# Sigmoid attention and a sigmoid-GELU MLP on one core: the first 512 tokens' x kept on chip, the left-over score step moved in among the previous unit's products with v, and decoding steps ranked by their load

## The chip, the cores and the metric

The kernel runs on one core of one Trainium2 chip. Its time is device microseconds of one execution, and the number that counts is the median of several runs. Beside the timed runs there is one execution under the hardware profiler; its instructions are what the profile shows.

The engines carry the profile's names: PE is TensorE's matmul, PEld its weight load, DVE is VectorE, ACT is ScalarE, SP is the engine from whose queue all DMAs are issued here.

## The reference

```
# q, k, v: (8, 12, 448, 64); w_in: (768, 2048); w_out: (2048, 768)
scores = q @ k.T / 8 - log(448)
attn   = sigmoid(scores) @ v                      # per batch and head
x      = attn, heads side by side                 # (3584, 768)
h      = x @ w_in
out    = (h * sigmoid(1.702 * h)) @ w_out
```

All of it is float32. The weights arrive as 64-bit words and are turned into float32 on chip.

## The kernel before, in words

**A planner writes the order.** The kernel first makes a list of tasks (`Plan.task`, line 101), each with an engine, a cost in microseconds, the tasks it depends on and the buffers it uses. `Plan.run` (line 113) then plays the list through by those costs and emits the instructions of each engine in the order that comes out. On the chip each engine works through its queue in that order and does not look past an instruction that waits. TensorE follows units of tasks in a given order: attention's are `side`, the rest `main`. ACT, DVE and SP pick, among the tasks that can begin, the one of the lowest key (line 226). A task's key is the place of its earliest user in the TensorE order (`keys`, line 278); `plan.early` sets the key of a listed task to half a place ahead of another one (line 141). A task of a higher key is put off when one of a lower key that is already on offer begins within 0.8 of its cost (lines 227 to 233). A task whose buffer has no slot yet may begin only when its key is within 14 places (`HORIZON`) of what TensorE is doing, unless it is marked `anytime` (line 166).

**Attention** (`attention`, line 701) has 48 pairs of heads (8 batches of 6) in 24 units of two pairs, so four heads. A pair's q and k come as one raw tile (`qkraw`, 5 buffers, loads at L432). DVE and ACT split it into a rounded part and a remainder (L458/L459 and L464, tiles `qk`, 2 buffers). The 448 keys make three chunks of 128 and 64 left over. A unit runs on TensorE, before the change, as

1. six score chunks, three per pair (`scores`, L593: three terms of two matmuls on 64x128 tiles of the array), each followed by a sigmoid on ACT (L579, tile `a`);
2. the left-over scores of all four heads (`scores_left`, L609: 64x64 tiles, straight from the two raw tiles), with their sigmoid into `al`, which has one buffer;
3. four products of score chunks with v (`values`, L626), the left-over's product (`values_left`, L639), and two more of L626. The first three chunks go to one v result, the last three to the other, and the left-over's product adds to both.

PSUM has four pairs of banks in attention, q0 to q3, and `two_banks(place)` (line 571) gives them out by place modulo 4. Before the change a unit's places are: score chunks 1 to 6, left-over 7, v results 8 and 9. So the left-over takes the banks of the third chunk, the first v result those of the fourth, and the fourth chunk of the next unit those of this unit's second v result.

`to_x` (line 656) empties a v result: ACT copies one half (L668) and DVE adds the other (L671) into a buffer `x32` of 448 tokens. A batch has 448 tokens and a block of the MLP 512, so every row of x is stored to DRAM (`xd`) in one or two parts, block by block. `make_x` (line 683) loads block 0's two halves of x back in three pieces each and splits them into rounded part and remainder (L458, L464). All other blocks are read back later.

**Decoding** (`decode`, line 476) takes 16 weight tiles from 64-bit words to float32. It goes on during attention: one load for every 2.9 pairs (`PACE`), two buffers of raw words, then seven to eight steps on DVE and ACT (L499 to L522), of which two take DVE 1.75 us each. Before the change a decoding step's key comes from the first use of its weights, which is in the MLP.

**The MLP** follows. `first_block` (line 811) does tokens 0 to 511 as plain products. The other six blocks go in two groups of three through a fast matrix scheme with fewer products (`triple`, line 951). All its matmuls stand at L799. The first weight pieces are split in `pieces` (line 817); the first two are marked `anytime`.

Of the kernel before, what the change touches and what calls it, by code (L numbers as in the profile page):

```python
# [19 lines left out]
P = 128  # L20
T = 512
# [3 lines left out]
WARM = 26  # L25

# [310 lines left out]
def sigmoid_attention_mlp(ctx: ExitStack, tc: tile.TileContext, qk, v, w, out):  # L337
# [138 lines left out]
    def decode(n):  # L476
# [47 lines left out]
        t_m.anytime = True  # L524
        decoded[n] = [Node(f, held(f, f"w32_{n}", NW_EL, k * NW_EL), [t_p]) for k in range(2)]
# [5 lines left out]
    spill = {n: [dram.tile([P, NJ, T], F32, name=f"xd{n}_{k}", tag=f"xd{n}_{k}") for k in range(2)] for n in range(NB)}  # L531
# [36 lines left out]

    place_of = {}
# [31 lines left out]
    def scores_left(n, sources, place):  # L601
# [12 lines left out]
        t = task("PE", 0.9, emit, [t for ts, _ in sources for t in ts], [ps, *(b for _, b in sources)])  # L614
        return t, sigmoid(f"a{n}_{NC}", a, ps, t, "al"), a

    def values(n, c, t_a, a, t_v, vr, ps):
# [13 lines left out]
        return task("PE", 0.76, emit, [t_a, t_v], [ps, a, vr])  # L631
# [23 lines left out]

    def to_x(b, p, ends, pair):

        xb = buffer("x32")
# [6 lines left out]
        for k, (t, ps) in enumerate(zip(ends, pair)):  # L665
            def lower(k=k, ps=ps):
                rows()
                nc.scalar.copy(xb.tile[:, k], ps.tile[:, 1, :S])  # L668

            c = task("ACT", act(S), lower, [t], [xb, ps])  # L670
            done.append(task("DVE", dve(S), lambda k=k, ps=ps: nc.vector.tensor_tensor(  # L671
                xb.tile[:, k], ps.tile[:, 0, :S], xb.tile[:, k], op=ALU.add), [c], [xb, ps]))
        copies.extend(done)
        for block, into, cols in places(b):
            for js in ([slice(0, 2)] if p % NJ < NJ - 1 else [slice(0, 1), slice(1, 2)]):
# [7 lines left out]
    def make_x(block, k):  # L683
        x = buffer("pair")
        n = NJ * T

        def first():
            if x.tile is None:
                make(x, "pair", [P, 2, 4, T], F32R, f"x{block}_{k}")

        t = [dma(lambda j=j: x.tile[:, 1, j].bitcast(F32), lambda j=j: spill[block][k][:, j], P * T * 4 / 1024,
                 spilled[block, k * NJ + j], [x], first) for j in range(NJ)]
        xs[block, k] = (round_and_rest(
            (act(n), cast(n), dve(n)), x, lambda: x.tile[:, 1, :NJ].bitcast(F32), t, [],
            lambda: x.tile[:, 0, :NJ], lambda: x.tile[:, 1, :NJ],
        ), x)
# [4 lines left out]
    def attention():  # L701
# [7 lines left out]
        units, held_ = [], 1  # L709
        for n, (b, p) in enumerate(pairs):  # L710
            t_q, qkr, t_v, vr = load_pair(b, p)
            t_s, s = split_pair(b, p, t_q, qkr)
            firsts.append(t_s)
            if n % 2:
                left = scores_left(n, [first, (t_q, qkr)], held_ + (7 if n > 1 else NC + 1))
            at = held_ + 1 + n % 2 * NC + (n == 1)
            chunks = [scores(n, c, [t_s] if n else t_q[: c + 1], s, at + c) for c in range(NC)]
            if n % 2 == 0:
                first, chunks0, pair0 = (t_q, qkr), chunks, (b, p)
                continue  # L720
            held_ += 9
            pair = [two_banks(held_ - 1), two_banks(held_)]
            both = [values(m, c, got[1], got[2], t_v, vr, pair[m % 2])
                    for m, cs in ((n - 1, chunks0), (n, chunks)) for c, got in enumerate(cs)]
            both.insert(NC + 1, values_left(*left[1:], t_v, vr, pair))
            copied = len(copies)
            to_x(*pair0, [both[NC + 1], both[-1]], pair)
            run = [t for t, _, _ in chunks0 + chunks]
            plan.early += [(t, run[1]) for t in urgent]
            urgent[:] = copies[copied:]  # L730
# [601 lines left out]
```

## Time and profile before

| what | us |
|---|---|
| timed runs | 1045.62, 1046.72, 1048.9 (median 1046.72) |
| the profiled execution's own time | 1042.55 |
| its span, first to last instruction | 1040.8 |
| PE busy | 1032.8 |
| DVE busy | 863.7 |
| ACT busy | 552.9 |
| matmuls of the MLP (L799), four groups of rows | 327.5 + 327.2 + 66.5 + 66.4 |
| products with v (L626) | 117.8 |
| score chunks (L593, split q and k) | 93.9 |

The granted clock of TensorE was 0.999. Busy times of different engines overlap, so they do not add up to the span. PE's ends are modelled, and matmuls overlap in the array, so a busy PE says little; where TensorE loses time, the starts of its instructions say more. A row of the timeline gives the start, the length until the last end, the engine, the line, the operation with its tiles, how many instructions were merged, and in brackets the idle time before it with what ended that. The rows of windows give, for a stretch, its length and each engine's busy time with the count of instructions in it.

### The profile page before, as it was taken

The numbers are of one execution on the slowest core, as the hardware profiler recorded it, in microseconds if no ns is written. First come the engines' busy times: TensorE is split into PE (matmuls) and PEld (weight loads), VectorE is DVE, ScalarE is ACT, GpSimd is POOL, SyncE is SP. The second block draws the span as 40 slices with busy tenths as digits, with TensorE's granted clock in tenths as the row PEclk, the third lists the DMA queues.
The fourth block names the chain that finished last, engine by engine and source line by source line (L and its number), as shares of the span: only waits on it lengthen the run. The fifth ranks groups of instructions, "written<-read, shape, count | busy, mean of one in ns | idle before, by whom it ended". The sixth has DMA issues, their size and how long they took to land.

```text
span 1040.8 us, 14831 instructions
## 1 busy us (share of the span) xinstructions
PE 1032.8 (99%) x5876; PEld 784.3 (75%) x5876; DVE 863.7 (83%) x792; ACT 552.9 (53%) x537; POOL 0.2 (0%) x4
## 2 busy tenths in 40 slices
PE   9999999999999999999999999999999999999998
PEld 5555555555888888888888888888888888888886
DVE  5999899984998857978998999889985658899856
ACT  6999889886655623435563443431325564233432
POOL 0000000000000000000000000000000000000000
PEclk9999999999999999999999999999999999999999
DMA  9999999973899998756676657878865555645466
GB/s 357 362 380 369 326 345 334 337 269 139 333 374 355 385 381 297 246 192 215 225 240 195 210 181 235 258 246 299 311 226 204 183 181 162 202 153 157 137 195 238
DMA packets 114708, 271.50 MB, mean 261 GB/s; under 512 B 10320, under 2 KB 80080, under 8 KB 112592
## 3 DMA queue, kind: packets, MB, share of 16 engines
q1 hardware_dynamic: 114640, 270.57, 74.8%
q8 instruction: 46, 0.75, 0.3%
q14 instruction: 22, 0.18, 0.0%
HBM read 185.60 MB, written 84.93 MB: 260 GB/s over the span
## 4 chain that ended last, share of the span: by engine, by line
PE 94%; DVE 2%; ACT 1%; DMA 1%; issue 1%; SPq 0%; ACTq 0%; DVEq 0%
PE p L799 63%; PE av L626 9%; PE sc L593 7%; PE h L799 6%; PE o_q L799 6%; PE sc L609 2%; PE av L639 1%; DMA qkraw<-qk 0%; DVE x L671 0%; ACT a L579 0%; DMA xd<-x 0%; ACT sign L503 0%; DVE w L522 0%; DVE qk L464 0%; DVE w L520 0%
## 5 line engine op out<-in xcount | busy, mean ns | idle before, releaser
L799 PE MATMUL p<-xp,w 128*128 128x512 f32 x1440 | 327.5, 389 | 0.1
L799 PE MATMUL p<-gp,w 128*128 128x512 f32 x1440 | 327.2, 389 | 0.0
L799 PEld LDWEIGHTS p<-xp,w 128*128 128x128 f32 x1440 | 270.2, 188 | 56.6 <-issue 0.5
L799 PEld LDWEIGHTS p<-gp,w 128*128 128x128 f32 x1440 | 270.3, 188 | 56.1
L579 ACT ACTIVATE a<-sc,bias 128x896 f32<-128x896 f32 x168 | 154.1, 1025 | 7.5 <-PE sc L593 7.3
L626 PE MATMUL av<-a,vraw 64*64 64x448 f32 x1152 | 117.8, 539 | 0.0
L593 PEld LDWEIGHTS sc<-qk 64*128 64x128 f32 x846 | 77.1, 184 | 26.5 <-issue 16.2
L593 PE MATMUL sc<-qk 64*128 64x448 f32 x846 | 93.9, 370 | 1.7 <-DVE qk L464 1.0
L626 PEld LDWEIGHTS av<-a,vraw 64*64 64x64 f32 x1152 | 42.2, 133 | 68.0 <-issue 48.3
L1197 ACT COPY h<-p 128x2048 f32<-128x2048 f32 x23 | 42.9, 1877 | 82.5 <-PE p L799 79.9
L1026 DVE TENSOR_TENSOR gp<-h,gp 128x2048 fp32r<-128x2048 f32 x27 | 61.8, 2287 | 6.8 <-ACT gp L1014 6.4
L799 PE MATMUL h<-x,w 128*128 128x512 f32 x288 | 66.5, 389 | 0.0
L799 PE MATMUL o_q<-g,w 128*128 128x512 f32 x288 | 66.4, 389 | 0.0
L1014 ACT CAST gp<-h 128x2048 fp32r<-128x2048 f32 x17 | 32.6, 1915 | 58.3 <-PE p L799 56.7
L799 PEld LDWEIGHTS h<-x,w 128*128 128x128 f32 x288 | 54.0, 188 | 11.9 <-DVE x L671 0.7
L799 PEld LDWEIGHTS o_q<-g,w 128*128 128x128 f32 x288 | 54.1, 188 | 11.2
L1231 DVE TENSOR_TENSOR h<-h,p 128x2048 f32<-128x2048 f32 x23 | 52.0, 2282 | 6.5 <-PE p L799 5.6
L1197 ACT COPY o<-p 128x1536 f32<-128x1536 f32 x18 | 25.7, 1445 | 55.3 <-PE p L799 55.1
L671 DVE TENSOR_TENSOR x<-av,x 128x448 f32<-128x448 f32 x48 | 29.9, 624 | 28.4 <-ACT x L668 28.1
L762 ACT CAST wc<-ws 128x384 fp32r<-128x384 f32 (+1 forms) x59 | 33.2, 577 | 37.4 <-DVE ws L742 19.4
L464 DVE TENSOR_TENSOR qk<-qkraw,qk 128x896 fp32r<-128x896 f32 x47 | 50.4, 1086 | 0.5
L1231 DVE TENSOR_TENSOR o<-o,p 128x1536 f32<-128x1536 f32 x18 | 31.3, 1751 | 13.9 <-PE p L799 12.9
(110 smaller groups left out, 1031.4 us busy)
## 6 DMA issues: line engine op xcount, KB each, us to landing
w<-c SPq DMA_DIRECT2D x140, 384.0 KB, 4.3
w<-c SPq DMA_DIRECT2D x52, 768.0 KB, 4.3
w<-w SPq DMA_DIRECT2D x16, 1536.0 KB, 9.4
c<-wc SPq DMA_DIRECT2D x56, 384.0 KB, 4.7
qkraw<-qk SPq DMA_DIRECT2D x47, 448.0 KB, 6.0
vraw<-v SPq DMA_DIRECT2D x24, 448.0 KB, 6.9
c<-wc SPq DMA_DIRECT2D x14, 768.0 KB, 5.0
c<-w SPq DMA_DIRECT2D x28, 384.0 KB, 3.9
```

What stands on the lines that cost most here:

```text
L464: lambda: nc.vector.tensor_tensor(lo(), src(), hi().bitcast(F32), op=ALU.subtract),
L579: nc.scalar.activation(a.tile, ps.tile[:, :, :S], AF.Sigmoid, bias=bias, scale=scale)
L593: nc.tensor.matmul(ps.tile[:, j, :S], lhsT=src[kk][rows, S + c * P : S + (c + 1) * P], rhs=src[qq][rows, :S], start=i == 0, stop=i == len( ...
L609: nc.tensor.matmul(ps.tile[cols, j, :S], lhsT=src.tile[rows, S + NC * P :], rhs=src.tile[rows, :S], start=True, stop=True, skip_group_chec ...
L626: nc.tensor.matmul(ps.tile[cols, h, :S], lhsT=vr.tile[rows, at : at + D], rhs=a.tile[rows, j], start=c == 0, stop=c == NC - 1 and (n % 2 = ...
L671: done.append(task("DVE", dve(S), lambda k=k, ps=ps: nc.vector.tensor_tensor(xb.tile[:, k], ps.tile[:, 0, :S], xb.tile[:, k], op=ALU.add), ...
L762: t_hi = on_either((act(n), lambda: nc.scalar.copy(into()[:, 0], node.view())), (cast(n), lambda: nc.vector.tensor_copy(into()[:, 0], node ...
L799: nc.tensor.matmul(ps, lhsT=ws[:, a, c * P : (c + 1) * P], rhs=x[:, d, k], start=start and i == 0 and j == 0, stop=stop and i == len(todo) ...
L1014: t_hi = on_either((act(n), lambda: nc.scalar.copy(part(0)(), node.view())), (cast(n), lambda: nc.vector.tensor_copy(part(0)(), node.view())),
L1026: nc.vector.tensor_tensor(part(1)(), node.view(), part(0)().bitcast(F32), op=ALU.subtract)
L1197: t = on_either((act(self.n), lambda: nc.scalar.copy(view(), node.view())), (dve(self.n), lambda: nc.vector.tensor_copy(view(), node.view())),
L1231: nc.vector.tensor_tensor(view(), x.view(), y.view(), op=ALU.add if s0 == s else ALU.subtract)
```

## The change

Three things change at once.

1. **x of the first 512 tokens stays on chip.** Batch 0's rows, and the first 64 tokens of batch 1, are added straight into two slots (`x_kept`), and `make_x` splits them from there. No `xd` tile exists for block 0. Batch 1's rows are added in two parts: 64 tokens into the slot, 384 into `x32`.
2. **The next unit's left-over scores** are run between this unit's `values_left` and its last two `values`. The first unit runs its own as before, the last one has none to run. PSUM places become: chunks 1 to 6, first v result 7, the next unit's left-over 8, second v result 9. Costs in the plan are changed with it (0.76 for a left-over step among v products, 0.9 for the first v product after scores).
3. **Decoding steps** of a load that belongs to pair p get the key of pair p+8's split (`DUE`), where there is such a pair. The first two weight pieces lose `anytime`.

```
+DUE = 8
...
         t_m.anytime = True
+        if pair + DUE < len(firsts):
+            plan.early += [(t, firsts[pair + DUE]) for t in (t_e, t_s, t_b, t_x, t_g, t_m, t_l, t_p)]
...
-    spill = {n: [...] for n in range(NB)}
+    spill = {n: [...] for n in range(1, NB)}
...
     def scores_left(n, sources, place):
-        t = task("PE", 0.9, emit, [t for ts, _ in sources for t in ts], [ps, *(b for _, b in sources)])
+        t = task("PE", 0.76 if n > 1 else 0.9, emit, [t for ts, _ in sources for t in ts], [ps, *(b for _, b in sources)])
...
     def values(n, c, t_a, a, t_v, vr, ps):
-        return task("PE", 0.76, emit, [t_a, t_v], [ps, a, vr])
+        return task("PE", 0.76 if c or n % 2 else 0.9, emit, [t_a, t_v], [ps, a, vr])
...
+    kept = {}
+
+    def x_kept(k):
+        if k not in kept:
+            b = plan.slot()
+            kept[k] = b, held(b, f"x0_{k}", NJ * T), []
+        return kept[k][0]
+
     def to_x(b, p, ends, pair):
-        xb = buffer("x32")
+        xb = buffer("x32") if b else None
+        cut = slice(0, S) if not b else slice(0, T - S) if b == 1 else None
...
+            if cut:
+                into = slice(0, S) if not b else slice(S, T)
+                kept[k][2].append(add(lambda x0=x0, j=j, k=k, into=into: row_kept(x0, j, k, into), cut, [*{at: 0, x0: 0}, ps]))
+                copies.append(kept[k][2][-1])
+            if b:
+                cols = slice(cut.stop if cut else 0, S)
+                done.append(add(lambda n=n, cols=cols: xb.tile[:, n, cols], cols, [xb, ps]))
         copies.extend(done)
         for block, into, cols in places(b):
+            if not block:
+                continue
...
-    def make_x(block, k):
+    def make_x(k):
+        b, view, t = kept[k]
         x = buffer("pair")
...
-        t = [dma(lambda j=j: x.tile[:, 1, j].bitcast(F32), lambda j=j: spill[block][k][:, j], P * T * 4 / 1024,
-                 spilled[block, k * NJ + j], [x], first) for j in range(NJ)]
-        xs[block, k] = (round_and_rest(
-            (act(n), cast(n), dve(n)), x, lambda: x.tile[:, 1, :NJ].bitcast(F32), t, [],
+        xs[0, k] = (round_and_rest(
+            (act(n), cast(n), dve(n)), x, view, t, [b], part(0), part(1),
...
+        units, loaded_of, at, count = [], {}, 2, len(pairs) // 2
+        for u in range(count):
+            got = sources(u)
+            if not u:
+                left = left_of(0, at + NC)
+            chunks = []
+            for i, (t_q, _, _, _, t_s, s) in enumerate(got):
+                n = 2 * u + i
+                chunks.append([scores(n, c, [t_s] if n else t_q[: c + 1], s, at + c) for c in range(NC)])
+                at += NC + (not n)
+            t_v, vr = got[0][2:4]
+            here, following = left, []
+            average = [two_banks(at)]
+            if u < count - 1:
+                left = left_of(u + 1, at + 1)
+                following = [left[0]]
+                at += 1
+            average.append(two_banks(at + 1))
+            at += 2
...
+            both[NC + 1 : NC + 1] = [values_left(*here[1:], t_v, vr, average), *following]
...
-            unit = [*run, left[0], *both] if n > 1 else [*run[:NC], left[0], *run[NC:], *both]
+            unit = [*run[:NC], *([] if u else [here[0]]), *run[NC:], *both]
...
                 t = split_piece(node, PIECE, into, b, first)
-                if count[0] < 2:
-                    for u in b.users:
-                        u.anytime = True
...
-        make_x(0, k)
+        make_x(k)
```

More of the change, by code (lines that the diff above doesn't have):

```diff
@@ L530, in sigmoid_attention_mlp @@
     xs = {}
-    spill = {n: [dram.tile([P, NJ, T], F32, name=f"xd{n}_{k}", tag=f"xd{n}_{k}") for k in range(2)] for n in range(NB)}
+    spill = {n: [dram.tile([P, NJ, T], F32, name=f"xd{n}_{k}", tag=f"xd{n}_{k}") for k in range(2)] for n in range(1, NB)}
     spilled, v_of = {}, {}
@@ L664, in to_x, with whole_row, row_kept, lower @@
         done = []
[L665 to L672, printed above, removed]
+        for n, (t, ps) in enumerate(zip(ends, pair)):
+            k, j = divmod(p + n, NJ)
+            x0 = x_kept(k) if cut else None
+            at = x0 if not b else xb
+            def whole_row(n=n, x0=x0, j=j, k=k):
+                if b:
+                    rows()
+                    return xb.tile[:, n]
+                return row_kept(x0, j, k, slice(0, S))
+            def row_kept(x0, j, k, cols):
+                return kept[k][1]()[:, j * T + cols.start : j * T + cols.stop]
+            def lower(whole_row=whole_row, ps=ps):
+                nc.scalar.copy(whole_row(), ps.tile[:, 1, :S])
+            c = task("ACT", act(S), lower, [t], [at, ps])
+            def add(into, cols, uses, whole_row=whole_row, ps=ps, c=c):
+                return task("DVE", dve(cols.stop - cols.start), lambda: nc.vector.tensor_tensor(
+                    into(), ps.tile[:, 0, cols], whole_row()[:, cols], op=ALU.add), [c], uses)
+            if cut:
+                into = slice(0, S) if not b else slice(S, T)
+                kept[k][2].append(add(lambda x0=x0, j=j, k=k, into=into: row_kept(x0, j, k, into), cut, [*{at: 0, x0: 0}, ps]))
+                copies.append(kept[k][2][-1])
+            if b:
+                cols = slice(cut.stop if cut else 0, S)
+                done.append(add(lambda n=n, cols=cols: xb.tile[:, n, cols], cols, [xb, ps]))
         copies.extend(done)
         for block, into, cols in places(b):
+            if not block:
+                continue
             for js in ([slice(0, 2)] if p % NJ < NJ - 1 else [slice(0, 1), slice(1, 2)]):
@@ L701, in attention, with sources @@
     def attention():
[L709 to L725, printed above, removed]
+        def sources(u):
+            if u not in loaded_of:
+                both = []
+                for b, p in pairs[2 * u : 2 * u + 2]:
+                    t_q, qkr, t_v, vr = load_pair(b, p)
+                    t_s, s = split_pair(b, p, t_q, qkr)
+                    firsts.append(t_s)
+                    both.append((t_q, qkr, t_v, vr, t_s, s))
+                loaded_of[u] = both
+            return loaded_of[u]
@@ L726, in attention @@
             copied = len(copies)
-            to_x(*pair0, [both[NC + 1], both[-1]], pair)
-            run = [t for t, _, _ in chunks0 + chunks]
+            to_x(*pairs[2 * u], [both[NC + 1], both[-1]], average)
+            run = [t for cs in chunks for t, _, _ in cs]
             plan.early += [(t, run[1]) for t in urgent]
             urgent[:] = copies[copied:]
-            unit = [*run, left[0], *both] if n > 1 else [*run[:NC], left[0], *run[NC:], *both]
+            unit = [*run[:NC], *([] if u else [here[0]]), *run[NC:], *both]
@@ L734, in attention @@
             units.append(unit)
-        place_of["next"] = held_ + 1
         return units
```

12 lines of the change are left out of this document (7 added, 5 removed).

## The prediction

> **What bounds the kernel now.** I read the page first, then windows over the stages, then the timeline of each engine in single units, and last the waits and the DMA issues. A unit is four heads: two pairs, two rounds of score products L593, one left-over score L609, and products with v (L626, L639).
>
> ```profile
> PE 1032.8 (99%) x5876; PEld 784.3 (75%) x5876; DVE 863.7 (83%) x792; ACT 552.9 (53%) x537; POOL 0.2 (0%) x4
> ```
> ```profile
> 16.19:251.67 235.48, 234.49 (x2305) 127.66 (x2301) 207.02 (x239) 209.92 (x238) 0.00 (x0) 1.00 0.90 328
> 251.67:1035.70 784.03, 783.88 (x3456) 648.52 (x3456) 650.76 (x544) 333.89 (x288) 0.00 (x0) 1.00 0.71 239
> 1035.70:1040.80 5.10, 0.00 (x0) 0.00 (x0) 0.00 (x0) 0.60 (x1) 0.00 (x0) 0.88 0.72 271
> ```
>
> The columns are length, then PE, PEld, DVE, ACT, POOL busy, clock, DMA share, GB/s. From 251.67 on, TensorE is idle 0.15 us in 784, at full clock, with instructions that the change leaves alone. The 5.1 us tail is untouched too. So any change of time must come from attention. The first of its 24 units ends at 16.19, and the window above holds the other 23: 235.48, or 10.24 each. PE looks full there as well, but its ends are modelled, so I measure starts. First a unit late in attention:
>
> ```profile
> 231.29 3.91 PE L593 MATMUL sc<-qk 64*128 64x448 f32 x36
> 235.13 0.98 PE L609 MATMUL sc<-qkraw 64*64 64x448 f32 x8
> 236.02 3.24 PE L626 MATMUL av<-a,vraw 64*64 64x448 f32 x32
> 239.08 0.93 PE L639 MATMUL av<-a,vraw 64*64 64x448 f32 x8
> 239.83 1.68 PE L626 MATMUL av<-a,vraw 64*64 64x448 f32 x16
> 241.44 1.89 PE L593 MATMUL sc<-qk 64*128 64x448 f32 x16
> ```
>
> Start to start it takes 10.15: scores 3.84, left-over 0.89, products with v 5.42. Now part of a unit whose scores had been held up:
>
> ```profile
> 100.23 2.09 PE L593 MATMUL sc<-qk 64*128 64x448 f32 x18 [0.46 <-DVE x L671]
> 102.25 0.98 PE L609 MATMUL sc<-qkraw 64*64 64x448 f32 x8
> 103.06 3.19 PE L626 MATMUL av<-a,vraw 64*64 64x448 f32 x32
> ...
> 108.43 2.12 PE L593 MATMUL sc<-qk 64*128 64x448 f32 x18
> ```
>
> Here the left-over takes 0.81 and the products 5.37, together 0.13 less for the same instructions. What the slower unit waits for shows in its sigmoids and weight loads:
>
> ```profile
> 234.06 1.01 ACT L579 ACTIVATE a<-sc,bias 128x896 f32<-128x896 f32 x1
> ```
> ```profile
> 234.95 1.01 ACT L579 ACTIVATE a<-sc,bias 128x896 f32<-128x896 f32 x1
> ```
> ```profile
> 236.02 0.21 PEld L626 LDWEIGHTS av<-a,vraw 64*64 64x64 f32 x8 [0.68 <-ACT a L579]
> ```
> ```profile
> 101.33 1.08 ACT L579 ACTIVATE a<-sc,bias 128x896 f32<-128x896 f32 x1
> ```
>
> The first two rows are the third and fourth sigmoid of their unit. The fourth ends at 235.96, and the first v product starts 0.06 later: it writes the unit's eighth pair of PSUM banks, and with four pairs in turn that is the one the fourth score chunk used. In the held-up unit the fourth sigmoid ends at 102.41, and the product starts 0.65 later: no wait. So a unit with nothing to wait for takes 3.84 + 0.81 + 5.37 = **10.02**, and 23 of them 230.5: attention holds 5.0 us of stalls. Two stretches divide them:
>
> ```profile
> 180.51:241.44 60.93, 60.93 (x604) 33.30 (x600) 52.30 (x61) 51.63 (x59) 0.00 (x0) 1.00 0.79 281
> 77.15:129.52 52.37, 51.43 (x505) 27.95 (x501) 47.35 (x53) 48.08 (x54) 0.00 (x0) 1.00 0.97 348
> ```
>
> The first has six units of 10.155, 0.13 over the floor: the PSUM wait alone. The second has five of 10.47, 0.45 over. With six units like these (6 x 0.45 = 2.7) and 17 like those (17 x 0.13 = 2.2) the 5.0 is accounted for; I put **2.2** to the PSUM wait and **2.8** to scores held up, where the waits name VectorE:
>
> ```profile
> PEld sc L593 <- DVE x L671: 2.2, 4, 0.8
> PE sc L593 <- DVE qk L464: 1.0, 2, 0.7
> ```
>
> **Part 1: the left-over scores move.** In the new order a unit is scores, four v products, left-over product with v, the next unit's left-over scores, two v products. No instruction is added: unit 0 gains a left-over, the last unit loses one, 0.75 to 0.81 each, net 0. PSUM places turn so that the first v product now follows the third score chunk's sigmoid. In the rows above that one ends at 235.07, 0.06 before L609 starts today, which uses the very same banks. So the 0.13 goes. Late next is this third sigmoid, with hardly any slack, but L609 meets it today at no cost. The moved step takes the banks of the fourth chunk, long read by then. **-2.2 us**; bounds: 0 if something as late replaces it, -2.2 if nothing does.
>
> The step adds a wait: the left-over scores need both raw q,k tiles of the next unit some 2.3 us before that unit starts (itself and two v products, 0.75 each by 239.08 to 239.83); two v products and the next unit's scores are queued behind it on TensorE.
>
> ```profile
> 46.73 3.85 PE sc L593 x36
> ```
> ```profile
> 31.19 1.11 SPq L432 DMA_DIRECT2D qkraw<-qk  x2
> ```
> ```profile
> qkraw<-qk SPq DMA_DIRECT2D x47, 448.0 KB, 6.0
> ```
> ```profile
> DVE qk L459 <- DMA qkraw<-qk: 6.3, 2, 5.8
> ```
>
> In the chain of waits a unit starts at 46.73; by the timeline of the DMA queue its second tile is issued at 31.19, lands in about 6 and is wanted at 44.4: 7 us spare. Waits on these loads occur twice, and sum to 6.3 us; the tile buffers now come free earlier. Cost 0; the worst wait of the row, 5.8, bounds one accident.
>
> The move has a second effect. VectorE adds the two halves of both v results (L671), and score chunk four waits for the second add:
>
> ```profile
> 240.61 0.62 DVE L671 TENSOR_TENSOR x<-av,x 128x448 f32<-128x448 f32 x1 [1.90 <-ACT x L668]
> 242.15 0.63 DVE L671 TENSOR_TENSOR x<-av,x 128x448 f32<-128x448 f32 x1 [0.91 <-ACT x L668]
> ```
> ```profile
> 118.42 0.62 DVE L671 TENSOR_TENSOR x<-av,x 128x448 f32<-128x448 f32 x1
> 118.95 1.75 DVE L522 SCALAR_TENSOR_TENSOR w<-w,expo 128x1536 f32<-128x1536 f32 x1
> 120.62 0.62 DVE L671 TENSOR_TENSOR x<-av,x 128x448 f32<-128x448 f32 x1
> ```
> ```profile
> 76.40 0.65 DVE L671 TENSOR_TENSOR x<-av,x 128x448 f32<-128x448 f32 x1
> 76.93 1.77 DVE L464 TENSOR_TENSOR x<-x 128x1536 fp32r<-128x1536 f32 x1
> 78.60 0.65 DVE L671 TENSOR_TENSOR x<-av,x 128x448 f32<-128x448 f32 x1
> ```
>
> Undisturbed, the adds start 1.54 apart, and the second ends at 242.78, 0.58 before the scores begun at 241.44 are half done (1.92 later). Where a 1.75 us step slips between them they are 2.20 apart, and the second is 0.66 late. With a left-over step (0.75) put between the two results, the natural distance becomes 2.29, so one such step fits. A shorter step first and a long one behind it still collide. I let half of the 2.8 us go, **-1.4**; bounds: -2.8 (all go) and, for new collisions, +5.2 (worked out under the rivals).
>
> **Part 2: x of block 0 stays on chip.** Fourteen DMAs go, among them:
>
> ```profile
> x<-xd SPq DMA_DIRECT2D x6, 256.0 KB, 6.2
> ```
>
> The queue that loses them made nobody wait but the two casts above, at the start: 0. The 12 rows of batch 1 are each added in two pieces instead of one. VectorE's price of a piece, from one operation at two sizes:
>
> ```profile
> L464 DVE TENSOR_TENSOR qk<-qkraw,qk x47: 1071/1085/1102, 7.5 to 237.6; 128x896 fp32r<-128x896 f32 x47
> ...
> L464 DVE TENSOR_TENSOR x<-x x2: 1748/1762/1775, 76.9 to 89.0; 128x1536 fp32r<-128x1536 f32 x2
> ```
>
> (1762 - 1085)/640 = 1.06 ns an element, which leaves 137 ns fixed. Twelve extra are 1.6 us of VectorE in units 3 to 5. Six are on the add that scores wait for: at most 6 x 0.14 = 0.8 us of PE, and 0 where that add has its 0.58 to spare. I take **+0.2**. ACT's copies stay as they are. Two slots of eleven stay taken until both x tiles are split, which now waits for no reload; eight decoded weights fit beside them: 0.
>
> **Part 3: ranks.** No instruction changes. Decoding steps of a load at pair p rank ahead of pair p+8, so older ones go first and the x split falls behind them. Attention's steps still go ahead, being at most two pairs on: 0, bounded by the same collisions. The first two weight pieces lose their freedom to run at any time; their splits move into the last unit, beside an idle VectorE:
>
> ```profile
> 240.00:260.00 20.00, 20.00 (x155) 12.84 (x146) 6.48 (x9) 12.12 (x15) 0.00 (x0) 1.00 0.33 121
> ```
>
> Cost 0. Without that cover the first MLP matmul would wait for two remainders of 768 elements, by the price above 0.95 each: 1.9.
>
> **Sum**: -2.2 - 1.4 + 0.2 = **-3.4 us**. The profiled execution took 1042.55 (span 1040.8 and 1.75 around), so it becomes 1039.15; the median of the timed runs, 1046.72, lies 4.2 above it and goes to **1043.3**. About 0.3%, 3.1 us, is what a measurement of this kernel can tell from no change.
>
> **Rivals.** (a) *Only the PSUM wait goes*: collisions stay at 2.8 because VectorE is as full (47.35 busy of 52.37) in shorter units. -2.2 + 0.2 gives 1044.7. For it: nothing in the change takes a step off VectorE. (b) *Everything goes*: floor units, -5.0, 1041.7. For it: 2.29 against 2.20; against: long steps behind short ones. (c) *The order gives nothing*: the 0.13 is the price of changing the array from 64x128 to 64x64 tiles, which every unit still does once each way, and collisions stay: 1046.7. Against it: the held-up unit changes tiles just the same and takes 0.81. The Trainium skill, TensorEngine Tiling (Array Packing), "Key Properties", says that switching the tiling mode drains TensorE; by that rule the switch cannot be moved away, and the gain of part 1 would be 0 if the 0.13 were the drain. The trace speaks against that last step: both units shown make the same two switches, and the 0.13 stands in one of them only. (d) *Slower*: decoding steps, now ranked ahead and met by more adds, collide in most units. Price: a held-up unit of the second stretch loses some 0.5. Sixteen decodings with one collision each are 8.0, against 2.8 today: +5.2 - 2.2 = +3.0, 1049.7. It decides from ten collisions in 23 units, where 5.0 is lost again; 2.8 means five or six today.
>
> **How the numbers follow.** Forecast (half the collisions gone) 0.42; (a) 0.25; (b) 0.15; (c) 0.10; (d) 0.08. The range reaches from (b), with 0.3 for a shift of the median (the three runs spread over 3.3), to (c) with the same: 1041.4 to 1047.0; (d) is left out, and some of the tails. Faster by over 0.3% (below 1043.6): (b), most of the forecast, which lies close to that bound, and a little of (a): 0.15 + 0.30 + 0.05 = 0.50. Slower: (d), less its mild cases: 0.07. The rest is 0.43.
>
> **What would show it.** Right: no L626 start waits on L579; first v product 3.84 behind the unit's first score; units of 10.02; attention ending near 248.3 with TensorE idle in no later stage; adds 2.2 to 2.3 apart. Wrong: units of 10.15 with the wait at another bank; "sc L593 <- DVE x L671" above 2.2 us; a gap ahead of the first L799 or a wait for raw q,k.

## The result, and the profile after

| | before | after |
|---|---|---|
| timed runs, first comparison (six each) | 1046.17 (1043.1 to 1048.9) | 1039.68 (1039.21 to 1041.93) |
| ratio of that comparison | | 0.9949 [0.9935, 0.9964] |
| again, nine and five runs | 1045.13 (1043.84 to 1046.89) | 1040.19 (1039.64 to 1040.73) |
| ratio of that comparison | | 0.9950 [0.9936, 0.9964] |
| span of the first profiled execution | 1040.8 | 1037.6 |
| first matmul of the MLP starts | 251.59 | 247.66 |

The changed kernel is faster by 0.5%, about 5 us. The prediction said 1043.3 with 1041.4 as its lowest: the sign was right, the size was not. Two runs of before that stood beside later experiments took 2101.7 and 3715.4 us and are in no ratio here. In the changed kernel score chunks stand at L594, left-over scores at L610, products with v at L627 and L640, sigmoids at L580, ACT's copies of x at L690, VectorE's adds at L695, the MLP's matmuls at L849.

The page's row of busy times and three windows (attention but its last two units, those two, the MLP; columns as in the prediction):

```profile
PE 1029.5 (99%) x5876; PEld 786.6 (76%) x5876; DVE 864.5 (83%) x805; ACT 550.1 (53%) x530; POOL 0.2 (0%) x4
```
```profile
17.20:227.36 210.16, 210.16 (x2105) 118.54 (x2102) 191.32 (x230) 186.40 (x210) 0.00 (x0) 1.00 0.88 318
227.36:247.65 20.29, 19.54 (x196) 11.04 (x192) 18.03 (x23) 17.30 (x19) 0.00 (x0) 1.00 0.63 224
247.65:1032.40 784.75, 784.26 (x3460) 648.47 (x3456) 649.22 (x545) 336.31 (x289) 0.00 (x0) 1.00 0.71 242
```

The first window holds 21 units: 210.16 / 21 = 10.008 each, without one unit held up. Before, 23 units had taken 10.24 each. The second window has 0.75 us of idle TensorE. In the third, the MLP's 3456 matmuls start 0.2266 us apart where nothing disturbs them. Wherever two starts lie more than 0.24 apart, the excess over 0.2266 is counted as lost: the first profile of before loses 0.5 us in all, this one 1.3. TensorE's timeline of one unit:

```profile
207.34 3.90 PE L594 MATMUL sc<-qk 64*128 64x448 f32 x36
211.18 3.24 PE L627 MATMUL av<-a,vraw 64*64 64x448 f32 x32
214.23 0.93 PE L640 MATMUL av<-a,vraw 64*64 64x448 f32 x8
214.99 0.93 PE L610 MATMUL sc<-qkraw 64*64 64x448 f32 x8
215.74 1.68 PE L627 MATMUL av<-a,vraw 64*64 64x448 f32 x16
217.35 3.90 PE L594 MATMUL sc<-qk 64*128 64x448 f32 x36
```

Start to start, the unit takes 10.01: scores 3.84, products with v 3.05 + 0.76 + 1.61, the next left-over scores 0.75. The fourth sigmoid of this unit, on ACT:

```profile
210.94 1.02 ACT L580 ACTIVATE a<-sc,bias 128x896 f32<-128x896 f32 x1
```

It ends at 211.96, and the first v product has started at 211.18: that product no longer waits for it. The one unit that is still held up takes 11.03 (227.36 to 238.39). TensorE, then VectorE at that place:

```profile
227.36 2.08 PE L594 MATMUL sc<-qk 64*128 64x448 f32 x18
230.19 2.10 PE L594 MATMUL sc<-qk 64*128 64x448 f32 x18 [0.75 <-ACT a L580]
238.39 3.91 PE L594 MATMUL sc<-qk 64*128 64x448 f32 x36
```
```profile
226.23 0.62 DVE L695 TENSOR_TENSOR x<-av,x 128x448 f32<-128x448 f32 x1
226.77 1.75 DVE L523 SCALAR_TENSOR_TENSOR w<-w,expo 128x1536 f32<-128x1536 f32 x1
228.43 0.61 DVE L695 TENSOR_TENSOR x<-av,x 128x448 f32<-128x448 f32 x1
228.97 1.08 DVE L465 TENSOR_TENSOR qk<-qkraw,qk 128x896 fp32r<-128x896 f32 x1
```

A 1.75 us step lies between the two adds, and the second add ends at 229.04, before the first 18 score matmuls end (227.36 + 2.08 = 229.44). The add is in time. Late is what stands behind it, the remainder of the second pair's q and k (L465, to 230.05), which the fourth score chunk reads; the start at 230.19 follows it. The bracket names ACT, and a sigmoid does end near there, at 230.17. But in the program this chunk waits for two things only: this remainder, and ACT's copy of x, which was over at 228.03. The weight load for the chunk also began at 230.16, before that sigmoid's end. So the named releaser is not the one that was waited for. In the list of TensorE's waits this one therefore stands under ACT:

```profile
PE sc L594 <- DVE qk L465: 0.9, 1, 0.9
PE sc L594 <- ACT a L580: 0.8, 1, 0.8
PE o_q L849 <- DVE w L815: 0.5, 1, 0.5
```

The first row is a wait at 8.98, in the first unit, and the second is the one at 230.19. No wait of scores for an add of x is left, here or in the list of the weight loads; before, it was 2.2 us in 4.

### The profile page after: what moved, and what is told of

Read it like the earlier page. It is cut to its first block, busy times and chain, and to the rows that moved or that the text cites. A ratio compares the mean times of both kernels' runs of the same rounds, so it can differ in the third digit from the quotient of the medians.

```text
span 1037.6 us, 14814 instructions
## 1 busy us (share of the span) xinstructions
PE 1029.5 (99%) x5876; PEld 786.6 (76%) x5876; DVE 864.5 (83%) x805; ACT 550.1 (53%) x530; POOL 0.2 (0%) x4
## 4 chain that ended last, share of the span: by engine, by line
PE 87%; DVE 5%; DMA 5%; ACT 1%; issue 1%; SPq 0%; ACTq 0%; DVEq 0%
PE p L849 63%; PE av L627 11%; PE sc L594 9%; DMA c<-wc 2%; PE av L640 2%; PE sc L610 2%; PE o_q L849 2%; DVE ws L792 2%; DVE wc L815 1%; DMA wf<-f 1%; DVE w L815 1%; DMA qkraw<-qk 1%; DMA xd<-x 1%; DVE g L465 0%; ACT w L812 0%
## 5 line engine op out<-in xcount | busy, mean ns | idle before, releaser
L849 PE MATMUL p<-xp,w 128*128 128x512 f32 x1440 | 327.3, 389 | 0.0
L849 PE MATMUL p<-gp,w 128*128 128x512 f32 x1440 | 327.2, 389 | 0.0
L849 PEld LDWEIGHTS p<-xp,w 128*128 128x128 f32 x1440 | 270.3, 188 | 56.2
L849 PEld LDWEIGHTS p<-gp,w 128*128 128x128 f32 x1440 | 270.3, 188 | 56.1
L580 ACT ACTIVATE a<-sc,bias 128x896 f32<-128x896 f32 x168 | 156.4, 1015 | 17.1 <-PE sc L594 9.4
L627 PE MATMUL av<-a,vraw 64*64 64x448 f32 x1152 | 118.1, 540 | 0.0
L594 PEld LDWEIGHTS sc<-qk 64*128 64x128 f32 x846 | 77.7, 184 | 24.2 <-issue 16.2
L594 PE MATMUL sc<-qk 64*128 64x448 f32 x846 | 92.2, 367 | 1.7 <-DVE qk L465 0.9
L1244 ACT COPY h<-p 128x2048 f32<-128x2048 f32 x25 | 46.5, 1876 | 88.6 <-PE p L849 86.1
L627 PEld LDWEIGHTS av<-a,vraw 64*64 64x64 f32 x1152 | 41.6, 133 | 60.8 <-issue 48.0
L849 PE MATMUL o_q<-g,w 128*128 128x512 f32 x288 | 66.8, 390 | 0.5 <-DVE w L815 0.5
L849 PE MATMUL h<-x,w 128*128 128x512 f32 x288 | 66.9, 390 | 0.0
L849 PEld LDWEIGHTS o_q<-g,w 128*128 128x128 f32 x288 | 54.0, 188 | 12.3 <-DVE w L815 0.8
L849 PEld LDWEIGHTS h<-x,w 128*128 128x128 f32 x288 | 53.9, 188 | 12.3 <-DVE x L695 0.7
L465 DVE TENSOR_TENSOR qk<-qkraw,qk 128x896 fp32r<-128x896 f32 x47 | 50.2, 1085 | 0.9 <-ACT qk L459 0.4
L695 DVE TENSOR_TENSOR x<-av,x 128x448 f32<-128x448 f32 (+2 forms) x54 | 30.3, 571 | 22.6 <-ACT x L690 22.0
```

The lines of the kernel that those rows point to most:

```text
L465: lambda: nc.vector.tensor_tensor(lo(), src(), hi().bitcast(F32), op=ALU.subtract),
L580: nc.scalar.activation(a.tile, ps.tile[:, :, :S], AF.Sigmoid, bias=bias, scale=scale)
L594: nc.tensor.matmul(ps.tile[:, j, :S], lhsT=src[kk][rows, S + c * P : S + (c + 1) * P], rhs=src[qq][rows, :S], start=i == 0, stop=i == len( ...
L627: nc.tensor.matmul(ps.tile[cols, h, :S], lhsT=vr.tile[rows, at : at + D], rhs=a.tile[rows, j], start=c == 0, stop=c == NC - 1 and (n % 2 = ...
L695: return task("DVE", dve(cols.stop - cols.start), lambda: nc.vector.tensor_tensor(into(), ps.tile[:, 0, cols], whole_row()[:, cols], op=AL ...
L849: nc.tensor.matmul(ps, lhsT=ws[:, a, c * P : (c + 1) * P], rhs=x[:, d, k], start=start and i == 0 and j == 0, stop=stop and i == len(todo) ...
```

## Experiments

The theory after the result: order (the left-over between the two results) takes away both the PSUM wait and the collisions. Its rivals: the rank does it, by moving long steps from between the adds; x on chip does it, by taking away the reload; the 0.13 belongs to the change of tile shape; and, since 6.5 us of medians stand against 3.2 us of spans, the difference is not what one profile of each shows. Three quantities are read from each trace: the start of the first MLP matmul ("attention ends"), what the MLP loses, counted as above ("MLP loses"), and the end of the last decoding step.

| kernel | median | ratio to before | attention ends | MLP loses | decoding ends |
|---|---|---|---|---|---|
| before, again; the last two profiles are single executions | 1045.0 | 0.9993 [0.9979, 1.0007] | 253.9, 253.3, 252.4 | 1.9, 0.5, 0.1 | 238.4, 237.7, 236.8 |
| after, again; the first profile is a single execution | 1040.19 | 0.9950 [0.9936, 0.9964] | 247.3, 247.4 | 2.5, 2.5 | 250.3, 250.4 |
| order_only | 1040.65 | 0.9954 [0.9940, 0.9967] | 248.7 | 1.4 | 253.5 |
| rank_only | 1042.54 | 0.9971 [0.9953, 0.9989] | 249.3 | 3.6 | 233.8 |
| x_only | 1043.29 | 0.9989 [0.9977, 1.0002] | 250.7 | 1.4 | 235.1 |
| rank_x | 1043.66 | 0.9991 [0.9983, 1.0000] | 250.3 | 2.0 | 234.8 |
| order_x | 1044.89 | 0.9996 [0.9985, 1.0007] | 247.8 | 5.3 | 254.9 |
| order_rank | 1041.7 | 0.9967 [0.9952, 0.9983] | 248.6 | 2.2 | 251.6 |
| left_early | 1040.88 | 0.9956 [0.9940, 0.9973] | 249.5 | 1.1 | 233.2 |
| banks_swapped (one execution) | 1040.9 | | 249.0 | 1.6 | 234.6 |
| dma_more | 1057.81 | 1.0133 [1.0117, 1.0149] | 247.4 | 19.2 | 250.4 |
| pace_27 | 1043.7 | 0.9989 [0.9978, 0.9999] | 248.6 | 4.5 | 243.2 |
| due_6 | 1041.26 | 0.9972 [0.9961, 0.9982] | 250.4 | 0.5 | 251.9 |
| due_10 | 1040.57 | 0.9969 [0.9956, 0.9981] | 247.7 | 3.0 | 253.7 |
| due_12 | 1045.7 | 1.0006 [0.9994, 1.0017] | 246.6 | 8.5 | 260.1 |

The medians of before that were timed beside these kernels went from 1043.81 to 1046.17, so kernels are compared by the ratio.

**The kernels themselves, again** (no edit). before_again:

> The kernel before, unchanged. Its profiled execution took 1042.55 us, its timed runs 1043.1 to 1048.9. Theory 1, the clock: the granted TensorE clock is lower in the long runs, about 0.001 of clock for each us, and the stages of the profile stay as they are. Theory 2, a wait that varies: at a clock of 0.999 the spans still differ by 3 us and more, and a profile of a long run shows longer units in attention or waits in the MLP that the first profile does not have. Theory 3, the profile itself: profiled executions lie near 1042.5 each time, timed ones near 1046.

before_p3, before_p4 and after_p2, one execution each:

> The kernel before, for a third profile of it. Its second had a span of 1044.6: ACT waited 2.44 us for the reload of x at 74 to 77, one unit took 12.68, and the MLP lost 1.9. Theory 1, the first profile (1040.8) was a lucky one: this one has a span of 1042 to 1045, ACT waiting 1 to 3 us for the reload, and 1 to 2 us lost in the MLP by waits for weights. Theory 2, the second was the unlucky one: a span near 1041, no wait for the reload.

> The same once more, for a fourth profile: the two theories expect the same of it as of the third.

> The changed kernel, for a second profile. With nothing reloaded in attention, both theories expect units of 10.01, the same one unit of 11.0, attention ending within 0.3 us of 247.7, and a span of 1037 to 1039.

after_again:

> The changed kernel once more, unchanged, in five rounds beside the kernel before: how large is the difference of the medians? If the first comparison (six runs of each, 1046.17 and 1039.68, so 6.5 apart) was typical, the medians lie 6 to 7 apart again, ratio 0.994. If a good part of it came from few runs of before with a slower clock (runs of before at a granted clock of 0.999 or more had a median of 1044.8, and the two profiles of after read 1039.4 and 1040.4), the medians lie 4 to 5 apart: 1044.8 against 1040, ratio 0.9955 to 0.996. If the profiled executions taken for the prediction were typical, 3.2 apart: ratio 0.997. Attention's units: 10.01 each but one or two, attention ending 247.3 to 247.7.

Measured: before is not one time. Its four profiled executions took 1042.55, 1046.42, 1044.27 and 1043.0; the one that the prediction rests on is the fastest. The three of after took 1039.4, 1040.37 and 1040.19. The main place where before differs from itself is the reload of x. ACT's timeline at the first half's rounding, in before's first profile, in before_again, and in x_only, which has no reload:

```profile
74.45 1.48 ACT L458 CAST x<-x 128x1536 fp32r<-128x1536 f32 x1
75.83 0.52 ACT L668 COPY x<-av 128x448 f32<-128x448 f32 x1
```
```profile
76.81 1.48 ACT L458 CAST x<-x 128x1536 fp32r<-128x1536 f32 x1 [2.44 <-DMA xd<-x]
78.19 0.52 ACT L668 COPY x<-av 128x448 f32<-128x448 f32 x1
```
```profile
74.52 1.71 ACT L503 ACTIVATE sign<-w 128x1536 bf16<-128x1536 int16 x1
76.08 0.57 ACT L689 COPY x<-av 128x448 f32<-128x448 f32 x1
```

In the first the reload had landed and nobody waited. In before_again ACT stands 2.44 us before the cast, and the copy behind it in ACT's queue is late by as much; VectorE's add waits for the copy, and scores for the add, in before_again's timelines of VectorE and TensorE:

```profile
78.75 0.62 DVE L671 TENSOR_TENSOR x<-av,x 128x448 f32<-128x448 f32 x1 [1.28 <-ACT x L668]
```
```profile
79.43 0.88 PE L593 MATMUL sc<-qk 64*128 64x448 f32 x6 [0.80 <-DVE x L671]
81.63 2.08 PE L593 MATMUL sc<-qk 64*128 64x448 f32 x18 [1.32 <-DVE x L671]
```

The other two profiles wait 1.41 and 0.82 at the same cast. The unit there takes 10.34 in the first profile, 12.67 in before_again, 11.64 and 11.04 in the others, and 10.14 in x_only. So the wait exists, and its size varies from run to run. Beside it, only one unit differs by more than 0.1 between the four profiles: at 171 us it takes 11.15 in before_p3 and 10.34 to 10.38 in the others.

**One part, or two, of the change.** order_only has the third group of the diff (the next unit's left-over, the PSUM places, the two costs) and nothing else; x_only has `x_kept`, the split adds and no `anytime`; rank_only has only

```
+DUE = 8
...
+        if pair + DUE < len(firsts):
+            plan.early += [(t, firsts[pair + DUE]) for t in (t_e, t_s, t_b, t_x, t_g, t_m, t_l, t_p)]
```

and the other three are the pairs of these. One detail does not pair up: `anytime` on the first two weight pieces is kept in order_only and rank_only and is missing in the other four.

> Only the new order of the left-over scores, with its PSUM places and plan costs; x goes through DRAM and decoding steps have no rank, as before. Theory 1, the order does it all: units of 10.01 us, sc waits for DVE x near zero, the end of attention 3.5 to 4 us earlier, ratio 0.995. Theory 2, the order takes only the PSUM wait away: no wait of L626 for L579, but three to six units still held up by VectorE, 2.8 us in sum, so 2.2 us earlier, ratio 0.998. Theory 3, the order gives nothing: units of 10.15.

> Only the rank of the decoding steps. Theory 1, the rank mends what x on chip costs and is nothing by itself: ratio 0.999 to 1.001, units of 10.15, four to six held up. Theory 2, the rank takes collisions away: none or one unit held up, ratio 0.998.

> Only x of block 0 on chip: old order, no rank. Theory 1, the reload of x is what makes the runs of before differ and what puts them above its first profile: no unit over 11 us, the runs at full clock lie within 1.5 us of each other, and attention ends 1 to 2 us earlier than in a typical run of before, unless the MLP gives it back. Theory 2, x on chip gains nothing without the rank, as it did with the order alone (5.3 us lost in the MLP): ratio 1.000 to 1.002 with 3 us or more lost there.

> Everything but the order: x of block 0 stays on chip, decoding steps have their rank, the left-over scores stand where they stood. Theory 1, the order does it all: units of 10.15, four to six units held up by VectorE, ratio 0.999 to 1.001. Theory 2, rank or x took the collisions away: units of 10.15 but none held up, 1 to 2.5 us earlier, ratio 0.998. If the spread of the timed runs came from the reload of x, the runs of this kernel lie within 1 us of each other.

> Order and x on chip, without the rank of the decoding steps. Theory 1, the order does it all: as the changed kernel, units of 10.01, at most one held up, ratio 0.995. Theory 2, the rank took the collisions away: three to six units held up by VectorE, ratio 0.997.

> Order and rank, with x of block 0 through DRAM as before. The run without rank, with order and x, ended attention at 247.8 but lost 5.3 us in the MLP, where the order alone lost 1.4 and the full change 1.3. Theory 1, x on chip holds two slots, decoding falls behind for it, and the rank only mends that: without x on chip the rank has nothing to mend, ratio 0.994 to 0.996 as with the order alone, MLP losses of 1 to 2 us. Theory 2, the rank is a gain of its own: decoding ends earlier than with the order alone, ratio 0.993 or less.

Measured: a unit of these kernels that isn't held up takes 10.00 to 10.02 with the new order, and 10.09 to 10.25 with the old one, mostly 10.16. So the 0.13 goes with the order, and with nothing else. Held up are units of 10.50 in order_only (three), of 10.48, 10.50 and 10.73 in order_x, of 10.85 in rank_x, of 11.00 and 11.05 in order_rank (the late remainder again), none beyond 10.46 in x_only and none in rank_only. The parts do not add: order alone brings about as much as all three; order with x ends attention as early as all three do and then loses it all in the MLP, 5.3 us. Without the order, the gains of x_only and rank_x are not clear of the noise, and rank_only gains 0.3%.

**Which of the two theories on the 0.13.** banks_swapped exchanges the PSUM places of the first v result and the moved left-over, so that the first v product follows the fourth sigmoid again:

```
-            average = [two_banks(at)]
+            average = [two_banks(at + (u < count - 1))]
...
-                left = left_of(u + 1, at + 1)
+                left = left_of(u + 1, at)
```

> The changed kernel with two PSUM places exchanged: the first v result takes the banks of the fourth score chunk, the moved left-over scores those of the third. Theory 1, the first v product waits for the sigmoid of the chunk whose banks it takes: that sigmoid ends 0.9 us after the third, so each of 23 units grows by 0.85 to 0.95, about 20 us in all, with waits of L627 for L580. Theory 2, the 0.13 was the price of changing the array's tiles: units stay at 10.01, no change of time.

Measured: units of 10.04, so 0.03 and not some 0.9, beside four held up (10.25 to 10.52). The edit did not do what it was meant to: the planner also exchanged the third and the fourth sigmoid in ACT's order, so the chunk that the product waits for was again the third to be read. The run decides nothing between bank and tile shape. What decides it is the series above: all kernels change from 64x128 to 64x64 tiles and back once a unit, at 10.01 and at 10.15 alike.

**Which of the two theories on the collisions.** left_early keeps everything but puts the moved left-over ahead of `values_left`, so that nothing lies between the ends of the two v results, and the adds are as near to each other as before:

```
-            both[NC + 1 : NC + 1] = [values_left(*here[1:], t_v, vr, average), *following]
+            end = values_left(*here[1:], t_v, vr, average)
+            both[NC + 1 : NC + 1] = [*following, end]
...
-            to_x(*pairs[2 * u], [both[NC + 1], both[-1]], average)
+            to_x(*pairs[2 * u], [end, both[-1]], average)
```

> The changed kernel with the moved left-over scores ahead of the left-over product with v, not behind it. PSUM places stay; the two adds of the v results are then due 1.5 us apart again, not 2.3. Theory 1, the longer distance between the adds took the collisions away: three to six units held up by 0.3 to 0.8 us each, 1.5 to 3 us later than the changed kernel. Theory 2, something else did (the rank, or the plan's costs): units of 10.01 with at most one held up, no difference.

Measured: VectorE's timeline of left_early (adds cut in pieces there), its wait row, and VectorE's timeline of order_rank:

```profile
56.64 0.55 DVE L695 TENSOR_TENSOR x<-av,x 128x384 f32<-128x384 f32 x1
57.11 1.75 DVE L523 SCALAR_TENSOR_TENSOR w<-w,expo 128x1536 f32<-128x1536 f32 x1
58.77 0.68 DVE L695 TENSOR_TENSOR x<-av,x 128x64 f32<-128x64 f32 x2
```
```profile
PEld sc L594 <- DVE x L695: 2.4, 7, 0.6
```
```profile
96.04 0.62 DVE L672 TENSOR_TENSOR x<-av,x 128x448 f32<-128x448 f32 x1
96.57 1.75 DVE L523 SCALAR_TENSOR_TENSOR w<-w,expo 128x1536 f32<-128x1536 f32 x1
98.24 0.62 DVE L672 TENSOR_TENSOR x<-av,x 128x448 f32<-128x448 f32 x1
```

The rows look alike, 2.13 and 2.20 from add to add. The difference is what TensorE does meanwhile: in left_early the scores had begun at 56.99 and the second adds start 1.78 later; in order_rank they had begun at 97.19 and the second add starts 1.05 later. But the distance doesn't suffice for every case. VectorE's timeline of order_only, where the scores begin at 107.89:

```profile
106.30 0.62 DVE L669 TENSOR_TENSOR x<-av,x 128x448 f32<-128x448 f32 x1 [1.33 <-ACT x L666]
106.84 0.95 DVE L515 TENSOR_TENSOR expo<-expo,sign 128x1536 bf16<-128x1536 bf16 x1
107.83 1.76 DVE L522 SCALAR_TENSOR_TENSOR w<-w,expo 128x1536 f32<-128x1536 f32 x1
109.50 0.62 DVE L669 TENSOR_TENSOR x<-av,x 128x448 f32<-128x448 f32 x1
```

Here a 0.95 us step stands ahead of the long one, the adds are 3.20 apart, and the second starts 1.61 behind the scores. Counted over all units, a long step stands between the two adds, and the second add then comes too late (1.37 us or more behind the scores' start; all the others stand at 1.08 or less):

| | before | rank_only | left_early | order_only | order_x | order_rank | after, each of three |
|---|---|---|---|---|---|---|---|
| long step between | 4 | 0 | 7 | 5 | 4 | 5 | 2 |
| of these, too late | 4 | 0 | 7 | 4 | 2 | 0 | 0 |

With the short distance every long step is one too many. With the long distance a single one fits between the adds and a pair does not; and the rank, with the order, leaves no such pair. In the old order the rank by itself leaves no long step between the adds at all (rank_only, one profile), but there every unit still pays the 0.13. So both theories hold a part: in the changed kernel the distance makes room for one step, and the rank keeps a second one out.

An add in time is not yet a unit in time. Where the second add starts 1.05 to 1.08 behind the scores, as in one of the two cases of after and in two of the five of order_rank, the remainder queued behind it is late and the unit takes 11.0, which is 1.0 over the floor; the late adds of the table cost 0.2 to 0.8. Where the add starts 0.70 to 0.73 behind them, the unit stays at 10.01.

left_early ends attention 2 us later than after does, as the first theory expects (249.5 against 247.3 to 247.7). Its whole time doesn't show it: the ratio of 0.9956 lies within the interval of after's 0.9950, since its MLP loses 1.1 where after's loses 1.3 to 2.5.

**What it is given back to.** The MLP now loses 1.3 to 2.5 us. dma_more writes 768 KB to DRAM six times more (4.7 MB), each after one of the MLP's saves:

```
-    saved = {}
+    saved, twice = {}, []
...
+                if not m and len(twice) < 6:
+                    twice.append(dram.tile([P, 2 * NW_EL], F32, name=f"t{len(twice)}", tag=f"t{len(twice)}"))
+                    dma(lambda d=twice[-1]: d.rearrange("p (t c) -> p t c", t=2), lambda into=into: into().bitcast(F32), 2 * KB, [t], [b])
```

> The changed kernel with six of the split weight pieces that the first block stores to DRAM stored twice, the second time to a place that nobody reads: 6 x 768 KB = 4.7 MB more between 255 and 380, where the DMA engines are busy all the time at some 370 GB/s, so 12 to 13 us more of transfers. Theory 1, the MLP's first 140 us run as fast as the DMAs let them: most of it comes out as waits of the first products for weights, 5 to 12 us more in the MLP. Theory 2, the waits there come from how the plan places the splits, and the transfers have slack: less than 1 us more.

Windows of after over the two stretches that follow attention, and TensorE's waits in dma_more:

```profile
247.65:280.00 32.35, 32.35 (x145) 26.48 (x142) 26.86 (x38) 18.33 (x26) 0.00 (x0) 1.00 0.83 302
280.00:390.00 110.00, 109.51 (x482) 90.14 (x482) 90.90 (x137) 55.39 (x80) 0.00 (x0) 1.00 1.02 392
```
```profile
PE p L849 <- DVE xp L1076: 11.7, 1, 11.7
PE h L849 <- ACT w L812: 2.2, 1, 2.2
```

Measured: 4.7 MB at the window's 392 GB/s are 12.0 us. The MLP lost 16.7 to 17.9 us more than in the three profiles of after. The two waits shown make 13.9 of it, and, as shown below, some 2 us of half clock stand behind each. From 280 to 390 the DMA engines have no time to spare (1.02 in the window above; before has 1.01 and 375 GB/s there), so transfers that are added to that stretch cost their full time.

The other way to load it is the decoding's own timing. due_6, due_10 and due_12 change `DUE` from 8; pace_27 loads each weight earlier (`PACE` 2.9 to 2.7).

> The changed kernel with the decoding steps ranked at pair p+12, not p+8. Theory 1, what counts of the rank is that older decodings go before newer ones, and before the MLP's splits: with 12 that is the same, within 0.1% of the changed kernel, units of 10.01. Theory 2, the nearness of the rank counts: decoding falls behind as without a rank (order and x alone: 5.3 us lost in the MLP), 2 to 5 us later.

> The changed kernel with the decoding steps ranked at pair p+10. With 12 attention ran at its floor to 246.6, but the last decoding ended at 260.1 and the MLP waited 6.0 us for it at 254.7; with 8 attention ends at 247.4 and the decoding at 250.5. Theory 1, the two trade against each other: attention ends at 247 or a little before, the decoding between 250 and 260, and the time lies between 1040 and 1046. A better one than the changed kernel only if the decoding ends by 252.

> The changed kernel with the rank at pair p+6. Theory 1, the trade: decoding ends no later than 250.5 and the MLP loses 0.5 to 1.5, but decoding steps now come ahead of splits and adds more often, one to four units held up, so 1039.5 to 1042. Theory 2, the MLP's loss does not follow the decoding any more, since the DMAs are the limit between 280 and 390: its loss stays at 1.3 to 2.5 whatever the decoding does.

> The changed kernel with a decoding load every 2.7 pairs, not 2.9, so that the last decoding, which ended at 250.7, 3 us behind attention, ends some 10 us earlier. Theory 1, the late decoding makes the MLP's first splits late: the waits at 256 and 362 go, 0.5 to 1 us less, unless the denser decoding collides with adds. Theory 2, the waits of the MLP come from the DMAs: its losses stay at 1.3 to 2.5 us.

Measured: with DUE at 6, 8, 10 and 12 attention ends at 250.4, 247.3 to 247.7, 247.7 and 246.6, and the MLP loses 0.5, 1.3 to 2.5, 3.0 and 8.5. due_12 is the purest case, with no unit held up: 22 take 10.00 to 10.02, and the last, which has no left-over to run, 9.25. Its windows across the end of attention, and TensorE's wait:

```profile
246.50:254.70 8.20, 8.20 (x40) 6.68 (x36) 7.53 (x8) 3.06 (x4) 0.00 (x0) 1.00 0.94 367
254.70:260.90 6.20, 0.36 (x2) 0.00 (x0) 5.96 (x7) 3.87 (x4) 0.00 (x0) 0.80 0.29 117
260.90:265.10 4.20, 4.09 (x9) 2.94 (x10) 4.20 (x5) 1.57 (x3) 0.00 (x0) 0.50 1.02 313
```
```profile
PE h L849 <- issue: 5.9, 1, 5.9
```

VectorE is full (5.96 of 6.20) while TensorE stands. The row of waits names no releaser, but VectorE's order does: its last decoding step runs to 260.13, the first split of a weight for the MLP starts at 260.17, and TensorE goes on at 260.94. The stalls did not go, they moved behind attention. pace_27 has units of 10.79, 10.84 and 11.00 again and waits 1.8 us in the MLP. due_6 has three units of 11.03 to 11.28. No other value beat the changed kernel.

## Why the prediction was right in sign and wrong in size

1. **PSUM wait, -2.2: right.** Units of 10.01 against the forecast 10.02, first v product 3.84 behind the first score, fourth sigmoid no longer waited for; the same in the three other kernels of parts with this order and in none without it. Rival (c) falls: if a change of tile shape drains TensorE, as the Trainium skill, TensorEngine Tiling (Array Packing), "Key Properties", has it, then that is part of the 10.01 and not the 0.13, since the kernels at 10.01 make as many changes.
2. **Collisions, -1.4: too small.** All of the 2.8 went: four late adds, and one late remainder (the unit of 10.67, whose wait of 0.35 names qk L464). The other 0.67 in the row for qk L464 that the prediction showed stands in the first unit, at 8.73, outside the 23. The reason for halving, "a shorter step first and a long one behind it still collide", is just what order_only shows, four times. What it left out is part 3: it gave the rank no effect on collisions but a bad one (d), and the rank removed these pairs. One new collision of 1.0 came at another place: the second pair's remainder, queued behind the second add. It nets -1.8. So (a) falls, and so does (d), of whose collisions one came, at 1.0, and not sixteen; (b) is nearest, with 22 of 23 units at the floor.
3. **Split adds, +0.2:** hardly seen; of units 3 to 5, one (unit 5) takes 10.08 and 10.09 in two of the three profiles of after, and none is above 10.02 in the first.
4. **Reload of x, 0: the step that failed.** "The queue that loses them made nobody wait" was read from one execution. In three of four it makes ACT wait 0.8 to 2.4 us, and attention ends at 252.8 in the mean of the four and not at 251.6: another 1.2, of which the unit of the reload makes 1.1 (mean 11.42 against 10.34). x_only, which lacks the reload, gains 1.1 (0.9989 of 1045), but its interval reaches past 1, so it doesn't confirm the size.
5. **MLP, 0: failed too, the other way.** "So any change of time must come from attention" took the MLP's full TensorE as a property of the MLP. The mean loss rises from 0.75 (four profiles) to 2.1 (three): +1.3. In all three of after most of it stands at 362 to 364 us, where TensorE waits for a split of weights, and the split waits for a load of those weights in the stretch where the DMA engines are full. From the chain of waits of the first profile, and from its list of waits:

```profile
354.34 7.12 DMA wf<-f
363.42 16.40 PE o_q L849 x71
```
```profile
ACT w L812 <- DMA wf<-f: 5.7, 2, 4.9
```

The load is issued at 354.34 and lands at 361.46; ACT has then stood idle for 4.9 us, and starts the split at 361.53. From 280 to 390 the three profiles of after move 391 to 392 GB/s, and the four of before 371 to 377. Decoding also ends later, at 250.7, behind attention, where before it ended at 236. That this makes the loss is not shown: rank_only loses 3.6 with decoding over at 233.8, and due_6 loses 0.5 with decoding over at 251.9, behind its attention. Only in due_12 is decoding itself seen to stand in the way.

In sum: -2.2 - 2.8 + 1.0 - 1.2 + 1.3 = -3.9; the mean spans of the four and three profiles, 1042.3 and 1038.2, differ by -4.1. The medians differ by 4.9; the other 0.8 is not explained, and four executions of a kernel whose runs spread over 3 to 9 us cannot settle it. That the first profiles agreed with the forecast so well (-3.2 against -3.4) was luck: in that pair the MLP's loss of 0.8 cancelled the 0.6 by which 2 and 3 came out better than forecast.

6. **From the profile to the median: failed.** Adding 4.2 to the profile's time took the three runs' median, 1046.72, as the level to start from. The forecast is 3.6 above the measured 1039.68. By the second comparison 1.6 of that is the base (1046.72 against 1045.13), 1.5 the change (4.9 against 3.4), and 0.5 the median of after (1040.19 against 1039.68). In one comparison or another, timed runs of before spread over 3 to 9 us and those of after over 1 to 3; the varying reload can be only a part of that, since x_only, without it, spreads over 5.0 (1041.87 to 1046.84).

Left open: why the load is issued so late in after, why the MLP's waits stand at other places in other kernels (the planner's whole list shifts with each edit), and the rest of before's spread.

## What to carry to other kernels

An in-order queue that has a wait for a reload in front of short, urgent work holds a stall that one profile may show as zero; profile the kernel before several times where the change removes a transfer, and take the typical one. When a stage is brought to its floor, look at what ended shortly before the stage's end, and at how full the next stage's transfers are: here decoding that used to be done 15 us ahead came to end behind attention, in due_12 it became the next stage's bound, and a late load took back part of the gain in the changed kernel. Order and rank each gained, and together they gained no more than order alone. Where a long step comes between two urgent ones, the distance between the urgent ones decides whether it does harm, and the order of the steps whether one or two stand there; the two are to be changed together, with an eye on what is queued behind the second urgent one.

## What the runs showed of the hardware that was not expected

A wait of TensorE can cost more than its length. Behind the 5.9 us wait in due_12 the granted clock is 0.50 for 4.2 us, in the last window above: 9 matmuls where 18 would fit, some 2 us more. The same follows the waits in dma_more, and even the shorter one of pace_27. In its windows TensorE is idle for 1.8 of 2.4 us and then gets through 11 matmuls in 4.1 us:

```profile
371.00:373.40 2.40, 0.57 (x4) 0.15 (x2) 1.62 (x2) 1.05 (x1) 0.00 (x0) 1.00 1.03 427
373.40:377.50 4.10, 4.10 (x11) 3.25 (x12) 1.00 (x1) 1.06 (x1) 0.00 (x0) 0.60 1.03 406
```

The waits of 0.75 us in after and of 1.3 us in order_x are followed by full clock. The Trainium skill, TensorE: Matmul & The Clock Gate, "What's actually happening", says that TensorE goes to half clock after an idle window of about 3.4 us and comes back after about as long a busy one. The half clock and the way back agree (0.50, 4.2 us); the length needed does not, since 1.8 us of idle time was followed by a mean of 0.60 here.
